# A hand-written order in place of a greedy scheduler for the attention and routing steps

## The chip, the core and the metric

The kernel runs on one core of one Trainium2 chip. The metric is the device time of one execution in microseconds, from the first to the last instruction and what lies around it. Three runs of the kernel before gave 416.49, 416.77 and 417.19 us.

## What is computed

Three layers follow one another. `A` is attention with a window of 64 keys over 2 batches, 8 heads, 576 positions and a head size of 64; its output is 1152 tokens of 512. `B` is a mixture of 8 experts: each token goes to the expert of its largest logit, in order of token up to 288 per expert, and its result is scaled by the softmax weight. `C` is a dense layer of 2048.

```python
scores = q @ k.T / 8; scores = where(0 <= i - j < 64, scores, -1e9)
x = softmax(scores) @ v                                # 1152 x 512
logits = x @ w_gate; e = argmax(logits); gate = softmax(logits)[e]
y = gate * (relu(x @ w1[e]) @ w2[e])                   # first 288 tokens of an expert
h = y @ w_in; out = (h * clip(h + 3, 0, 6) / 6) @ w_out
```

## The kernel before

**Stages.** Attention works on 9 blocks of 128 tokens (`j`), each in two halves of 64 queries (`g`, 18 of them). After five blocks an *early routing* picks one expert, the one most chosen so far, from the logits of the first 640 tokens, so that its weights are loaded and its tokens gathered while attention goes on. When all nine blocks are done the *late routing* places all tokens. Then TensorE works off the rest of the early expert's units, the teams of experts, and the dense layer. The order of everything from the early expert's remaining units on comes from a second planner in the same file with an estimate of its own; the change does not touch it.

**Steps of the first part.** Each is a node with a name, an engine or two it may run on, a cost, what it needs, a ring of buffers it takes from, and those that it frees:

- `lq`, `lk`, `lv` j: load 128 rows of q, k, v (256 KB each; block 4 crosses from one batch to the next, so its loads are two transfers). They are issued on SP's queue, one after the other, and so are `wg` (gate weights, two small transfers), `st` (store of a finished block) and `wl` u h (eight loads of 512 KB of the early expert's weights).
- `tq`, `tk`, `tv` j: TensorE turns the rows, four 128x128 products into one bank (L504). `eq`, `ek`, `ev`: ScalarE or VectorE copies the bank out (`copy`, L456 to L462).
- `s` j: 16 score products of 64x64 into two banks (L568). `m` g: VectorE adds the mask and takes the maximum, four instructions (L581). `e` g: four exponentials on ScalarE (L594). `pt` g: the turn of the result (L604); `ep` g: its copy.
- `cv0` to `cv2` j: GpSimd copies v into place (L486). `gw` j: the gate logits of v, four products (L534). `ew`, `tw`, `ex`: copied, turned (L548), copied beside v.
- `av` j: 16 products with the values (L622) into one pair of banks; `f` j: VectorE divides and sums up the logits (`finish`, L634 to L650).
- Early routing: `top` (`choose`, L130 to L138), `pp` (counts), `pl` (`early_expert`), `fl` (`early_flags`), `gE` (`early_gate`), `ix` and `ie` (index), `ga` (GpSimd gathers 128 rows), `sE`, `tE`, `xE` (scaled, turned, copied), `hotp`.
- The early expert: `e0`, `e1` u (two halves of the first product), `er` (relu), `et`, `eh` (turned, copied), `e2`, `e3` (second product).
- Late routing: `ch`, `cn`, `pL`, `rk`, `sa`, `px`, `sx`, `g0` (first gather), `gt`, `gc`, `hot`, `pg`, `sg`.

Rings matter where a step waits: `sp` (1) lets `s` j+1 begin only when both masks of block j are done; `p` (1) is the one bank of the `pt`; `x` (1) is one bank shared by `gw`, `tw`, `pp`, `ix`, `tE` and others; `t` (2) the two banks of the turns; `o` (1) the pair of banks of `av`.

**What sets the order.** `run_nodes` (L424) keeps a clock for each engine, looks at all nodes whose needs are met, and issues next the one with the smallest key: its start by the clock, a priority from the table `PRIO`, and its cost. Nodes with two engines get the one that comes out ahead. The engines then run their instructions in the order in which they were issued; each engine waits where an operand is not there.

Of the kernel before, what the change touches and what calls it, by code (L numbers as in the profile page):

```python
# [23 lines left out]
def tile_kernel(ctx, tc, q, k, v, w_gate, w1, w2, w_in, w_out, out, cap):  # L24
# [292 lines left out]
    GAP = -0.2  # L317
    EPS, CW, COLD, LAG = 0.015, 0.3, 6.0, 0.15
    PRIO = {'q': -30, 'k': -29, 'v': -27, 'tq': -7, 'eq': 8, 'tk': -10, 'ek': 3, 'cv': 1, 'tv': 1, 'ev': 2, 'gw': 1, 'ew': 1, 'tw': 1, 'ex': -4, 's': 2, 'm': 5, 'e': 2, 'pt': 2, 'ep': 9, 'av': 2, 'f': 8, 'st': 0, 'top': -5, 'tail': 2, 'ear': 78, 'hot': 60, 'gt': 25, 'fl': 13, 'ga': 58, 'xE': 5, 'turn': 20}
    CS = {'xE': 1.15, 'ep': 1.07, 'eq': 1.07, 'sE': 1.15, 'rk': 1.3, 'q': 1.15, 'v': 0.7}  # L320
    with ExitStack() as actx:
# [74 lines left out]
        nodes, done, emitted = {}, {}, []  # L396
# [3 lines left out]
        clock = dict.fromkeys(("PE", "A", "V", "P", "D"), 0.0)  # L400

        def node(name, prio, engs, fn, needs=(), take=None, free=(), lag=LAG):
            engs = {e: c * CS.get(name[0] if isinstance(name, tuple) else name, 1.0) for e, c in engs.items()}
            nodes[name] = (prio, engs, fn, needs, take, free, lag)

        def ready(name):
            _, _, _, needs, take, _, _ = nodes[name]
            r = 0.0
            for n in needs:
                if n not in done:  # L410
                    return None
                r = max(r, done[n])
            if take:
                order = taken[take]
                if len(order) >= rings[take]:
                    old = order[len(order) - rings[take]]
                    if freed.get((take, old), (0, 0.0))[0] < holders.get((take, old), 1):
                        return None
                    r = max(r, freed[take, old][1])
            return r  # L420

        holders, now = {}, [0.0]

        def run_nodes():  # L424
            while nodes:
                able = []
                for name, (prio, engs, *_) in nodes.items():
                    r = ready(name)
                    if r is None:
                        continue  # L430
                    for e, c in engs.items():
                        t = max(clock[e], r)
                        if e == "PE" and t < COLD:
                            c = 2 * c
                        key = (t + EPS * prio + (c if len(engs) > 1 else min(engs.values())) * CW, prio)
                        able.append((key, name, e, t, c))
                best = min(able)

                able = [a for a in able if a[3] + a[4] <= best[3] + GAP]
# [222 lines left out]
        node("wg", 6, {"D": 0.3}, lambda e: load_wg(), lag=2.0)  # L662
        node("rc", 30, {"P": 6.0}, lambda e: routing_constants())
        A_V = {"A": 0.5, "V": 0.6}
        for j in range(NJ):
# [20 lines left out]
            old = [("av", i) for i in (j - NV, j - NV + 1) if i >= 0]
            node(("ex", j), p + PRIO["ex"], {"A": 0.32, "V": 0.4}, x_out(j), [("tw", j)] + old, None, [("x", ("tw", j))])
            for g in (2 * j, 2 * j + 1):
                o = p + g % 2
# [184 lines left out]
        node("top", p, {"V": 0.8}, lambda e: choose(0, NE), [("f", j) for j in range(NE)] + ["rc"])  # L874
        node("pp", p, {"PE": 0.3}, early_counts, ["top"], "x")
        node("pl", p, {"V": 1.4}, early_expert, ["pp"], None, [("x", "pp")])
        node("fl", p + PRIO["fl"], {"V": 1.2}, early_flags, ["pl"])
        node("gE", p + PRIO["fl"], {"V": 1.35}, early_gate, ["fl"])
        node("ix", p + PRIO["fl"], {"PE": 0.2}, early_index, ["gE"], "x")
        node("ie", p + PRIO["fl"], {"V": 0.3}, early_index_out, ["ix"], None, [("x", "ix")])  # L880
        node("ga", p + PRIO["ga"], {"P": 1.04}, early_gather, ["ie"], lag=6.0)
        node("sE", p + PRIO["turn"], {"A": 0.48, "V": 0.4}, early_scale, ["ga"])
        node("tE", p + PRIO["turn"], {"PE": 0.44}, early_turn, ["sE"], "x")
# [1210 lines left out]
```

## Time and profile before

| | us |
|---|---|
| median of 3 runs (lowest, highest) | 416.77 (416.49, 417.19) |
| the profiled execution | 416.61 |
| its span, first to last instruction | 414.9 |
| PE busy | 400.3 (96% of the span) |
| DVE busy | 280.1 (68%) |
| ACT busy | 233.9 (56%) |
| POOL busy | 49.3 (12%) |

PE is TensorE, DVE VectorE, ACT ScalarE, POOL GpSimd, SP the engine that issues most transfers. The span is measured by the profiler inside one execution, so a change of the span by some us is one of the time. Matmuls are pipelined: the busy time of one is longer than the step from its start to the start of the next, and it is the steps that add up. The mean granted clock of TensorE over the span was 0.994 of full speed.

### The profile page before, as it was taken

What the parts mean: (1) busy time and instruction counts of PE and PEld (TensorE: products, weight loads), DVE (VectorE), ACT (ScalarE), POOL (GpSimd) and SP (SyncE); (2) the same over time, 40 slices, a digit from 0 to 9 for tenths busy, and PEclk for the clock granted to TensorE, in tenths of its full rate; (3) what the DMA queues carried; (4) which work ended last, traced back from release to release, by engine and by line L of the source; (5) the groups of instructions that cost most, each with busy time, mean ns of one, the idle gap of its engine ahead of it and who ended that gap; (6) DMA issues with size and microseconds to landing.
All of it is one profiled execution on the core that took longest, in us unless ns stands there. A gap on an engine that the chain in (4) does not pass through costs nothing.

```text
span 414.9 us, 8440 instructions
## 1 busy us (share of the span) xinstructions
PE 400.3 (96%) x3066; PEld 341.7 (82%) x3066; DVE 280.1 (68%) x781; ACT 233.9 (56%) x510; POOL 49.3 (12%) x109
## 2 busy tenths in 40 slices
PE   8999889999999999999999999999999999999992
PEld 5787666668999898898989999888888888999981
DVE  1988977599789789876789999358895222322430
ACT  3886863687586747666885566267573222322330
POOL 8733402030012000000000000000000000200111
PEclk9999999999999999999999999999999999999997
DMA  9999685987787999899700560033500000100101
GB/s 168 212 217 222 218 294 171 308 285 240 228 263 226 352 300 303 286 344 346 263 2 0 165 242 0 2 101 103 203 2 2 0 0 2 74 27 2 51 28 57
DMA packets 63842, 65.43 MB, mean 158 GB/s; under 512 B 30688, under 2 KB 47072, under 8 KB 63792
## 3 DMA queue, kind: packets, MB, share of 16 engines
q1 hardware_dynamic: 62224, 59.79, 46.4%
q0 software_dynamic: 1568, 5.01, 3.6%
q8 instruction: 26, 0.43, 0.4%
q14 instruction: 24, 0.20, 0.1%
HBM read 60.08 MB, written 4.72 MB: 156 GB/s over the span
## 4 chain that ended last, share of the span: by engine, by line
PE 90%; DVE 5%; ACT 2%; issue 1%; POOL 0%; POOLq 0%; ACTq 0%; DVEq 0%
PE banks L244 76%; PE banks L504 2%; PE banks L622 2%; PE banks L568 1%; PE banks L604 1%; DVE neg L581 1%; PE banks L1475 1%; PE banks L661 1%; PE banks L1500 1%; PE banks L534 1%; PE banks L1310 1%; ACT pe L594 1%; PE banks L1559 1%; PE banks L1408 0%; DVE xt L649 0%
## 5 line engine op out<-in xcount | busy, mean ns | idle before, releaser
L244 PE MATMUL banks<-x,wt 128*128 128x320 f32 (+3 forms) x432 | 79.8, 336 | 0.0
L244 PEld LDWEIGHTS banks<-x,wt 128*128 128x128 f32 x432 | 70.8, 188 | 7.1
L244 PE MATMUL banks<-wt,g 128*128 128x512 f32 x288 | 69.6, 390 | 0.0
L263 DVE TENSOR_TENSOR wt<-raw,wt 128x512 fp32r<-128x512 f32 x100 | 64.6, 685 | 4.9 <-ACT wt L258 4.6
L1621 DVE SCALAR_TENSOR_TENSOR gf<-r,banks 128x320 f32<-128x320 f32 (+3 forms) x48 | 26.6, 553 | 60.3 <-ACT r L1618 60.1
L1618 ACT ACTIVATE r<-banks,c_three 128x320 f32<-128x320 f32 (+3 forms) x48 | 27.9, 582 | 68.4 <-PE banks L244 68.2
L244 PEld LDWEIGHTS banks<-wt,g 128*128 128x128 f32 x288 | 53.7, 188 | 10.6
L258 ACT CAST wt<-raw 128x512 fp32r<-128x512 f32 x100 | 58.7, 628 | 4.5 <-PE banks L244 4.0
L244 PE MATMUL banks<-xT,wt 128*128 128x224 f32 (+2 forms) x288 | 38.2, 282 | 0.0
L244 PE MATMUL banks<-h,wt 128*128 128x224 f32 (+2 forms) x288 | 37.0, 279 | 0.0
L244 PEld LDWEIGHTS banks<-xT,wt 128*128 128x128 f32 x288 | 34.8, 191 | 1.6 <-issue 0.4
L244 PEld LDWEIGHTS banks<-h,wt 128*128 128x128 f32 x288 | 34.6, 192 | 0.8 <-issue 0.8
L1624 ACT CAST g<-gf 128x320 fp32r<-128x320 f32 (+2 forms) x40 | 21.3, 534 | 16.4 <-DVE gf L1621 16.4
L1627 DVE TENSOR_TENSOR g<-gf,g 128x320 fp32r<-128x320 f32 (+2 forms) x40 | 23.3, 584 | 10.1 <-ACT g L1624 9.4
L1664 POOL DMA_INDIRECT out_dram<-raw,cidx x4 | 3.9, 981 | 204.5 <-DVE raw L1658 196.9
L244 PE MATMUL banks<-x,wt_fixed 128*128 128x320 f32 (+3 forms) x144 | 26.8, 337 | 0.4 <-ACT x L1391 0.4
L244 PEld LDWEIGHTS banks<-x,wt_fixed 128*128 128x128 f32 x144 | 23.5, 188 | 3.0 <-ACT x L1391 0.7
L206 ACT ACTIVATE c<-raw 128x512 f32<-128x512 f32 x32 | 21.5, 673 | 6.2 <-DVE raw L229 4.7
L244 PE MATMUL banks<-wt_fixed,g 128*128 128x512 f32 x96 | 23.2, 390 | 0.0
L222 DVE SCALAR_TENSOR_TENSOR c<-raw,c 128x512 uint32<-128x512 uint32 x32 | 22.1, 690 | 0.8
L581 DVE CUSTOM_DVE_ANT_0 neg<-banks,tmask 128x128 f32<-128x128 f32 x72 | 16.2, 286 | 9.4 <-PE banks L568 9.4
L594 ACT ACTIVATE pe<-neg,nmx 128x128 f32<-128x128 f32 x72 | 22.3, 392 | 0.1
(310 smaller groups left out, 629.4 us busy)
## 6 DMA issues: line engine op xcount, KB each, us to landing
raw<-in_moe_w_dram SPq DMA_DIRECT2D x56, 512.0 KB, 5.9
raw<-in_moe_w_in_dram SPq DMA_DIRECT2D x16, 512.0 KB, 6.6
raw<-in_moe_w_out_dram SPq DMA_DIRECT2D x16, 512.0 KB, 6.1
early<-in_moe_w_dram SPq DMA_DIRECT2D x8, 512.0 KB, 6.6
x_dram<-xt SPq DMA_DIRECT2D x9, 256.0 KB, 2.8
q_sb<-in_q_dram SPq DMA_DIRECT2D x8, 256.0 KB, 3.9
k_sb<-in_k_dram SPq DMA_DIRECT2D x8, 256.0 KB, 4.8
v_sb<-in_v_dram SPq DMA_DIRECT2D x8, 256.0 KB, 4.5
```

The lines of the kernel that those rows point to most:

```text
L206: nc.scalar.activation(box["c"].bitcast(F32), box["hi"].bitcast(F32), AF.Abs)
L222: nc.vector.scalar_tensor_tensor(out=box["c"], in0=box["hi"], scalar=0xC0000000, in1=box["c"], op0=ALU.bitwise_and, op1=ALU.bitwise_or,)
L244: nc.tensor.matmul(out, l, r, start=(start and n == 0), stop=(stop and n == len(pairs) - 1))
L258: nc.scalar.copy(hi, r)
L263: V.tensor_tensor(out=lo, in0=r, in1=hi.bitcast(F32), op=ALU.subtract)
L504: nc.tensor.transpose(pt[:, hp, :], t[:, 2 * hp : 2 * hp + 2, :].rearrange("p h d -> p (h d)"), ident)
L581: V.tensor_tensor_reduce(out=neg[:, hp, :], in0=box["sp", g][:, hp, :], in1=tmask[:, first, :], scale=-1.0, scalar=3.0e38, op0=ALU.add, op ...
L594: nc.scalar.activation(pe[:, hp, :], neg[:, hp, :], AF.Exp, bias=nmx[:, hp : hp + 1], scale=-1.0)
L1618: nc.scalar.activation(r, ph, AF.Relu, bias=c_three)
L1621: V.scalar_tensor_tensor(out=gf, in0=r, scalar=6.0, in1=ph, op0=ALU.min, op1=ALU.mult)
L1624: nc.scalar.copy(hi, gf)
L1627: V.tensor_tensor(out=lo, in0=gf, in1=hi.bitcast(F32), op=ALU.subtract)
```

## The change

The greedy choice is gone. One string, `ATTENTION`, lists the 309 steps in the order in which they are issued, with `:a` or `:v` behind those that may run on ScalarE or VectorE. `run_nodes` goes through it word by word. Priorities, the tables `PRIO` and `CS`, the names `holders` and `GAP` and the counting of holders are gone; node costs are other numbers, and each engine's clock starts at another time. The steps themselves, their rings and their instructions are the same; 30 of the copies are on the other of their two engines.

```diff
-    GAP = -0.2
-    EPS, CW, COLD, LAG = 0.015, 0.3, 6.0, 0.15
-    PRIO = {'q': -30, 'k': -29, 'v': -27, 'tq': -7, ...
-    CS = {'xE': 1.15, 'ep': 1.07, 'eq': 1.07, 'sE': 1.15, 'rk': 1.3, 'q': 1.15, 'v': 0.7}
+    ATTENTION = """
+        lk.0 tk.0 ek.0:a lq.0 lv.0 cv2.0 lq.1 tq.0 lk.1 tv.0 eq.0:a s.0 m.0 m.1 lv.1 cv1.0 tq.1 ev.0:a eq.1:a wg
...
+        f.8 ch hotp.1 e0.1 e1.0 pL cn rk er.0:a e1.1 er.1:a hotp.3 et.0 et.1 st.6 eh.0:a e0.2 sa hot.6 e2.0 px hot.8
+        sx eh.1:v e3.0 e1.2 gt er.2:v e2.1 hot.5 hot.7 gc e3.1 g0 pg sg
+    """
...
-        clock = dict.fromkeys(("PE", "A", "V", "P", "D"), 0.0)
+        clock = {"PE": 5.0, "A": 1.3, "V": 1.2, "P": 7.1, "D": 2.9}
...
         def run_nodes():
-            while nodes:
-                able = []
-                for name, (prio, engs, *_) in nodes.items():
...
-                best = min([best] + able, key=lambda a: (a is best, a[0][1])) if able else best
-                _, name, e, t, c = best
-                _, _, fn, _, take, free, lag = nodes.pop(name)
+            name_of = {n if isinstance(n, str) else ".".join(map(str, n)): n for n in nodes}
+            for word in ATTENTION.split():
+                word, _, e = word.partition(":")
+                name = name_of.pop(word)
+                engs, fn, _, take, free, lag = nodes[name]
+                e = {"a": "A", "v": "V"}[e] if e else next(iter(engs))
+                t, c = max(clock[e], ready(name)), engs[e]
+                if e == "PE":
+                    if t < 7.1:
+                        c *= 1.95
...
                 if take:
                     taken[take].append(name)
                 now[0] = t
                 fn(e)
                 clock[e] = t + c
-                done[name] = t + c + lag
+                done[name] = t + c + (LAG[e] if lag is None else lag)
...
-            node(("s", j), o + PRIO["s"], {"PE": 0.93}, scores(j), needs, "sp", [("qd", ("eq", j))])
+            node(("s", j), {"PE": 0.9}, scores(j), needs, "sp", [("qd", ("eq", j))])
```

**VectorE, early routing.** The election of the early expert ends with `eI`; the rows of `neg` and `nmx` are a mask group (numbers tell the buffers apart). Before:

```order
L743 TENSOR_REDUCE e1_1_216<-e8_0_211 128x1
L744 TENSOR_SCALAR nsub_131<-subE_128 128x8
L745 CAST eI_222<-e1_1_216 128x1
L581 ISA neg_1001,nmx_1002<-banks_84,tmask_170 128x128
L581 ISA nmx_1002 128x1
```

Now:

```order
L744 TENSOR_REDUCE e1_1_216<-e8_0_211 128x1
L745 TENSOR_SCALAR nsub_131<-subE_128 128x8
L746 CAST eI_222<-e1_1_216 128x1
L756 TENSOR_TENSOR top_f_88<-oh_87,subE_128 128x40
L757 TENSOR_SCALAR capS_130<-subE_128 128x8
```

The flags follow the election at once; the mask groups that stood between `top`, `pl`, `fl` and `gE` stand ahead of `f.4` and `top`, except those of blocks 7 and 8, which stand behind `gE` as before.

**SP, the loads after the gate weights.** `wgb` is `wg`; a row with x2 and 64 partitions is a load of block 4 in two halves. Before:

```order
L359 DMA wgb_177<-in_moe_w_gate_dram 64x4x8 x2
L472 DMA q_sb_303<-in_q_dram 128x8x64
L472 DMA k_sb_327<-in_k_dram 128x8x64
L472 DMA v_sb_351<-in_v_dram 128x8x64
L472 DMA q_sb_378<-in_q_dram 128x8x64
L472 DMA k_sb_406<-in_k_dram 128x8x64
L472 DMA v_sb_441<-in_v_dram 128x8x64
```

Now:

```order
L373 DMA wgb_177<-in_moe_w_gate_dram 64x4x8 x2
L478 DMA k_sb_288<-in_k_dram 64x8x64 x2
L478 DMA k_sb_299<-in_k_dram 128x8x64
L478 DMA q_sb_337<-in_q_dram 128x8x64
L478 DMA q_sb_348<-in_q_dram 128x8x64
L478 DMA k_sb_365<-in_k_dram 128x8x64
L478 DMA v_sb_378<-in_v_dram 128x8x64
```

The loads k.4, k.2, q.2, q.3, k.3, v.2 stand where q.2, k.2, v.2, q.3, k.3, v.3 stood; v.3, q.4 and k.7 follow. Behind them SP has `lv.4 lk.5 lq.5 lv.5 lq.6 lk.8 st.0 lk.6 lq.7 st.1 st.2 lv.6 lv.7 lq.8 st.4 lv.8 st.3`, then seven of the weight loads `wl`, `st.5`, and the eighth.

**ScalarE, the end of attention.** `pe` are the exponentials of a half block, `pT` and `vT` copies of turned banks, `vx` and `vy` the copies `ex`, `c64` the scaling `sE` of the gathered rows. Before, the last instructions of attention:

```order
L460 COPY pT_1145<-banks_84 128x512
L460 COPY vT_1154<-banks_84 128x512
L594 ACTIVATE pe_1190<-neg_1173,nmx_1174 128x128 x4
L460 COPY vx2_187<-banks_84 128x8x8
L460 COPY vy2_190<-banks_84 64x8x8
L594 ACTIVATE pe_1218<-neg_1182,nmx_1183 128x128 x4
L460 COPY pT_1252<-banks_84 128x512
L594 ACTIVATE pe_1276<-neg_1246,nmx_1247 128x128 x4
L594 ACTIVATE pe_1285<-neg_1254,nmx_1255 128x128 x4
L462 ACTIVATE c64_1188<-c64_1188,sgE_133 128x512
L460 COPY pT_1310<-banks_84 128x512
```

Now:

```order
L466 COPY vT_1141<-banks_84 128x512
L600 ACTIVATE pe_1188<-neg_1083,nmx_1084 128x128 x4
L600 ACTIVATE pe_1193<-neg_1143,nmx_1144 128x128 x4
L466 COPY pT_1226<-banks_84 128x512
L600 ACTIVATE pe_1236<-neg_1181,nmx_1182 128x128 x4
L466 COPY pT_1241<-banks_84 128x512
L466 COPY vx1_186<-banks_84 128x8x8
L466 COPY vy1_189<-banks_84 64x8x8
L466 COPY vy2_190<-banks_84 64x8x8
L600 ACTIVATE pe_1260<-neg_1200,nmx_1201 128x128 x4
L468 ACTIVATE c64_1179<-c64_1179,sgE_133 128x512
L466 COPY pT_1305<-banks_84 128x512
```

Between the exponentials of the last four half blocks stand two copies `pT` (ep.14, ep.15) and the three of ex.7, where one `pT` and the two of ex.8 stood; the scaling `c64` is still ahead of the last `pT`.

## Rows read from the trace of the kernel before

**Rows 1.** The page's chain of work that ended last: shares by engine.

```profile
PE 90%; DVE 5%; ACT 2%; issue 1%; POOL 0%; POOLq 0%; ACTq 0%; DVEq 0%
```

**Rows 2.** Busy time by stretch (length; then busy of each engine, clock, DMA share, GB/s).

```profile
7.90:36.93 29.03, 28.56 (x483) 23.16 (x484) 23.85 (x128) 22.27 (x65) 15.11 (x45) 1.00 0.97 210
36.93:61.14 24.21, 20.90 (x362) 16.10 (x361) 20.99 (x140) 18.61 (x54) 6.67 (x12) 1.00 0.83 264
61.14:72.86 11.72, 10.82 (x77) 7.57 (x74) 8.27 (x45) 3.55 (x14) 3.33 (x5) 1.00 0.49 154
72.86:414.90 342.04, 333.70 (x2129) 291.39 (x2127) 226.59 (x467) 186.89 (x374) 17.71 (x17) 0.99 0.43 146
```

**Rows 3.** The chain in order of time, one block of attention (start, us, what).

```profile
20.45 1.18 PE banks L622 x32
...
22.22 0.87 PE banks L504 x8
23.09 1.03 PE banks L568 x32
...
24.71 0.35 PE banks L534 x8
25.07 0.59 PE banks L504 x4
25.66 0.16 PE banks L548
```

**Rows 4.** VectorE's timeline from the end of av.4 to the masks of block 7.

```profile
36.93 0.17 DVE L634 TENSOR_SCALAR rd<-banks 128x8 f32<-128x8 f32 x1 [0.68 <-PE banks L622]
...
38.40 0.20 DVE L130 TENSOR_REDUCE top_m<-logits 128x5 f32<-128x40 f32 x1
...
39.61 0.28 DVE L581 CUSTOM_DVE_ANT_0 neg<-banks,tmask 128x128 f32<-128x128 f32 x1
...
41.30 0.15 DVE L733 SCALAR_TENSOR_TENSOR e<-banks,c_desc 128x8 f32<-128x8 f32 x1
...
42.54 0.28 DVE L581 CUSTOM_DVE_ANT_0 neg<-banks,tmask 128x128 f32<-128x128 f32 x1
...
43.38 0.20 DVE L755 TENSOR_TENSOR top_f<-oh,subE 128x40 f32<-128x40 bf16 x1
...
45.11 0.28 DVE L581 CUSTOM_DVE_ANT_0 neg<-banks,tmask 128x128 f32<-128x128 f32 x1
...
45.95 0.19 DVE L770 TENSOR_REDUCE et<-ex 128x5 f32<-128x40 f32 x1
...
47.88 0.21 DVE L456 COPY vx<-banks 128x64 f32<-128x64 f32 x1
...
50.78 0.28 DVE L581 CUSTOM_DVE_ANT_0 neg<-banks,tmask 128x128 f32<-128x128 f32 x1
```

**Rows 5.** DMA issues around 6.3, 11.55, 12.94 and 51.2 us (last: us to landing).

```profile
wgb<-in_moe_w_gate_dram SPq DMA_DIRECT2D x1, 8.0 KB, 4.0
...
k_sb<-in_k_dram SPq DMA_DIRECT2D x1, 256.0 KB, 5.9
...
v_sb<-in_v_dram SPq DMA_DIRECT2D x1, 256.0 KB, 5.6
...
c<-x_dram,eI POOLq DMA_INDIRECT x1, 7.1
```

**Rows 6.** SP's timeline: the issues of the eleventh and twelfth load.

```profile
11.55 1.11 SPq L472 DMA_DIRECT2D k_sb<-in_k_dram  x1
12.94 0.87 SPq L472 DMA_DIRECT2D v_sb<-in_v_dram  x1
```

**Rows 7.** ScalarE's timeline from 45.48: exponentials of two half blocks, two copies.

```profile
45.48 2.45 ACT L594 ACTIVATE pe<-neg,nmx 128x128 f32<-128x128 f32 x8
47.83 0.56 ACT L460 COPY kT<-banks 128x512 f32<-128x512 f32 x1
48.30 0.59 ACT L462 ACTIVATE qd<-banks 128x512 f32<-128x512 f32 x1
```

More of the change, by code (lines that the diff above doesn't have):

```diff
@@ L392, in rows @@
                 o += n
-        nodes, done, emitted = {}, {}, []
+        nodes, done = {}, {}
         rings = {'q': 3, 'k': 4, 'v': 3, 'qd': NQD, 't': 2, 's': 2, 'sp': 1, 'p': 1, 'o': 1, 'x': 1, 'neg': 4, 'pe': 3, 'pT': 4, 'vT': 3, 'vw': 4, 'xt': 4}
@@ L399, in tile_kernel, with node @@
         freed = {}
-        clock = dict.fromkeys(("PE", "A", "V", "P", "D"), 0.0)
-        def node(name, prio, engs, fn, needs=(), take=None, free=(), lag=LAG):
-            engs = {e: c * CS.get(name[0] if isinstance(name, tuple) else name, 1.0) for e, c in engs.items()}
-            nodes[name] = (prio, engs, fn, needs, take, free, lag)
+        clock = {"PE": 5.0, "A": 1.3, "V": 1.2, "P": 7.1, "D": 2.9}
+        def node(name, engs, fn, needs=(), take=None, free=(), lag=None):
+            nodes[name] = (engs, fn, needs, take, free, lag)
         def ready(name):
-            _, _, _, needs, take, _, _ = nodes[name]
+            _, _, needs, take, _, _ = nodes[name]
             r = 0.0
             for n in needs:
-                if n not in done:
-                    return None
                 r = max(r, done[n])
@@ L415, in ready @@
                 if len(order) >= rings[take]:
[L416 to L419, printed above, removed]
-            return r
-        holders, now = {}, [0.0]
+                    r = max(r, freed[take, order[len(order) - rings[take]]])
+            return r
+        now, form = [0.0], [128]
+        FORMS = {"gw": 32, "s": 64, "av": 73}
+        LAG = {"PE": 0.2, "V": 0.14, "A": 0.15, "P": 0.1, "D": 1.5}
         def run_nodes():
-            while nodes:
-                able = []
-                for name, (prio, engs, *_) in nodes.items():
[L428 to L439, printed above, removed]
-                best = min([best] + able, key=lambda a: (a is best, a[0][1])) if able else best
-                _, name, e, t, c = best
-                _, _, fn, _, take, free, lag = nodes.pop(name)
+            name_of = {n if isinstance(n, str) else ".".join(map(str, n)): n for n in nodes}
[8 more added lines that the diff above has]
+                        c *= 1.95
+                    f = FORMS.get(word.split(".")[0], 128)
+                    if f != form[0]:
+                        form[0] = f
+                        c += 0.094
                 if take:
@@ L447, in run_nodes @@
                 clock[e] = t + c
-                done[name] = t + c + lag
+                done[name] = t + c + (LAG[e] if lag is None else lag)
                 for ring, owner in free:
-                    n, was = freed.get((ring, owner), (0, 0.0))
-                    freed[ring, owner] = n + 1, max(was, t + c + 0.1)
+                    freed[ring, owner] = max(freed.get((ring, owner), 0.0), t + c + 0.15)
+            assert not name_of, name_of
         def copy(e, out, in_, scale=None):
@@ L686, in tile_kernel @@
+            node(("gw", j), {"PE": 0.18}, v_gate(j), [("ev", j), "wg"], "x", [("vT", ("ev", j))])
+            node(("ew", j), {"A": 0.17, "V": 0.2}, w_out_(j), [("gw", j)], "vw", [("x", ("gw", j))])
+            node(("tw", j), {"PE": 0.11}, w_turn(j), [("ew", j)], "x", [("vw", ("ew", j))])
             old = [("av", i) for i in (j - NV, j - NV + 1) if i >= 0]
-            node(("ex", j), p + PRIO["ex"], {"A": 0.32, "V": 0.4}, x_out(j), [("tw", j)] + old, None, [("x", ("tw", j))])
+            node(("ex", j), {"A": 0.16 * parts, "V": 0.2 * parts}, x_out(j), [("tw", j)] + old, None, [("x", ("tw", j))])
@@ L702, in tile_kernel @@
                 needs += [("ex", j - 1), ("cv2", j - 1)]
-            node(("av", j), p + PRIO["av"], {"PE": 1.15}, values(j), needs, "o", free)
+            node(("av", j), {"PE": 1.1}, values(j), needs, "o", free)
             if j + 1 < NJ:
-                node(("f", j), p + PRIO["f"], {"V": 1.3}, lambda e, j=j: finish(j), [("av", j)], "xt", [("o", ("av", j))])
-                node(("st", j), p + PRIO["st"], {"D": 0.62}, lambda e, j=j: store_x(j), [("f", j)], None, [("xt", ("f", j))])
-            else:
-                node(("f", j), p + PRIO["f"], {"V": 0.85}, lambda e, j=j: finish(j), [("av", j)])
-        p = 10 * NE + PRIO["top"]
+                node(("f", j), {"V": 1.35}, lambda e, j=j: finish(j), [("av", j)], "xt", [("o", ("av", j))])
+                node(("st", j), {"D": 0.75}, lambda e, j=j: store_x(j), [("f", j)], None, [("xt", ("f", j))])
+            else:
+                node(("f", j), {"V": 1.0}, lambda e, j=j: finish(j), [("av", j)])
         A1E = ac.tile([128, NE, 128], F16, name="A1E")
@@ L872, in early_out @@
             copy(e, t, box["aE"])
[L874 to L883, printed above, removed]
+        node("top", {"V": 1.2}, lambda e: choose(0, NE), [("f", j) for j in range(NE)] + ["rc"])
+        node("pp", {"PE": 0.3}, early_counts, ["top"], "x")
+        node("pl", {"V": 1.25}, early_expert, ["pp"], None, [("x", "pp")])
+        node("fl", {"V": 1.75}, early_flags, ["pl"])
+        node("gE", {"V": 1.9}, early_gate, ["fl"])
+        node("ix", {"PE": 0.2}, early_index, ["gE"], "x")
+        node("ie", {"V": 0.3}, early_index_out, ["ix"], None, [("x", "ix")])
+        node("ga", {"P": 0.4}, early_gather, ["ie"], lag=6.0)
+        node("sE", {"A": 0.61, "V": 0.5}, early_scale, ["ga"])
+        node("tE", {"PE": 0.44}, early_turn, ["sE"], "x")
         node(
-            "xE", p + PRIO["xE"], {"A": 0.48, "V": 0.6}, lambda e: copy(e, xTE, box["tE"]), ["tE"], None,
+            "xE", {"A": 0.5, "V": 0.6}, lambda e: copy(e, xTE, box["tE"]), ["tE"], None,
             [("x", "tE")],
```

98 lines of the change are left out of this document (50 added, 48 removed).

## The prediction

> **What bounds the kernel now.** I read the chain of waits first, to see which engine the end hangs on: TensorE has 90% of it [rows 1]. Then the busy time in five stretches, cut where the chain changes hands [rows 2]. The reader should compare PE busy with the length of each stretch. From 72.86 us on TensorE is busy 333.70 of 342.04, and most of the rest is the last store. Between 7.90 and 36.93 it idles 29.03 − 28.56 = 0.47 us, between 36.93 and 61.14 it idles 3.31, between 61.14 and 72.86 it idles 0.90. The change reaches only what lies before 72.86: the instructions behind it stand as they stood. So the gain can come from two places: the 4.68 us of idling, and the returns of TensorE from another array shape, which [rows 3] price. Four 128x128 turns take 0.44 (the row of x8 is 0.87), but 0.59 when they follow the values, scores or gate products. That is 0.15 for each return.
>
> Third I read the timeline of VectorE from 36.93 [rows 4], because there DVE rows stand in the chain. The reader should see the early routing cut in slices: `top` at 38.40, two mask groups, `pl` at 41.30, a mask group, `fl` at 43.38, a mask group, `gE` at 45.95, and the next masks (m.14) only at 50.78. In these 12.38 us VectorE is the bound; TensorE, ScalarE and the loads wait for it.
>
> Below, a name such as m.14 is a step of the list: m masks of a half block, e exponentials, pt and ep turn and copy of them, s scores, av values, f finish, tq/tk/tv turns, ew/ex copies of the gate part.
>
> **The change, part by part.**
>
> *Durations, clocks, the removed priorities.* Nothing. With order and engine both written, no duration decides where an instruction stands.
>
> *Up to `top`.* Now 36.93 is where av.4 ends, and `top` starts at 38.40 [rows 4]. In the list av.4 has two more scores in front of it (s.5, s.6: 2 × 1.03), one single turn less (0.16) and three returns less (11 in place of 14, because s.3 gw.2 av.1, gw.3 av.2, gw.4 av.3 and s.6 gw.5 av.4 now stand side by side): 2.06 − 0.16 − 0.45 = +1.45 us, so 38.4 minus the idling of before that may vanish, about 37.9. Next the waits that the list makes. The gate weights are issued with the same place in the queue and land at 6.3 + 4.0 [rows 5]; gw.0 now stands right behind two turns and can begin at 10.05, so it waits 0.3 to 0.5. The loads k.4 (in two halves) and then k.2, q.2, q.3, k.3, v.2, v.3 follow the first six. The eleventh and twelfth load land at 11.55 + 5.9 = 17.45 and 12.94 + 5.6 = 18.54 [rows 5, 6], 1.09 apart; the 210 GB/s of [rows 2] make 262 kB in 1.25. I take 1.18, between them. Counted back, q.2 lands at 15.0 and q.3 at 16.2, and TensorE reaches them 0.3 us earlier each. Counted on, the eighteenth, q.5, lands at 25.6, where TensorE stands at 25.2: 0.4. With 0.3 behind the VectorE copy ew.0 I have 1.7 us of waits and av.4 ending at 39.6. VectorE has m.12 and m.13 in front of f.4, which end at 39.8; f.4 takes 1.47 (36.93 to 38.40), so `top` starts at 41.3, **+2.9 us**. Bounds: no wait at all gives 37.9 + 1.47 = 39.4, twice the waits 43. All later loads have slack: v.6 waits in SP's queue for the store behind f.2 (about 32.3), lands near 37 and is turned at 39.6; v.8 waits for the store behind f.4, lands near 45.5 and is turned at 49.5.
>
> *From `top` to m.14.* The four mask groups have gone in front of f.4, and the slices stand together. `top` 1.21 (38.40 to 39.61), ep.10 0.6 (no row of it here; ScalarE's copy of a tile of that size lasts 0.56 to 0.59 [rows 7]), 0.3 of waiting for the counts, `pl` 1.24, `fl` 1.73, `gE` 1.93 [rows 4]: 7.0 us in place of 12.38. Then m.14 starts at 48.3 instead of 50.78, **−5.4**. Cover: s.7 must be done by then. TensorE has 6.5 us of work from av.4 to s.7 by the prices of [rows 3], and waits about 1.1 us, because tw.6 and av.5 stand behind the bank that `pl` frees; s.7 ends at 47.2, a microsecond early.
>
> *From m.14 to the end of av.8.* Before, 50.78 to 61.14 = 10.36. What is late next is ScalarE. It has ep.12, ev.8, e.14, e.15, ep.14, e.16, ep.15, ex.7, e.17, sE, ep.17 in this order. A copy of a bank moves it on by 0.47 (47.83 to 48.30), two groups of exponentials by 2.35 (45.48 to 47.83) [rows 7]: 5 × 0.47 + 4 × 1.18 + about 1.15 for ex.7 and sE (0.59 is the longest copy of [rows 7]) = 8.2. ep.12 cannot start before TensorE has done pt.13, gw.7, tq.8 and pt.12 behind s.7, about 1.2 after m.14 starts. Behind ep.17 come its remaining length, a hop and av.8 (1.18): 1.4. About 0.9 is spent waiting, ev.8 for its turn and sE for the gathered rows. Sum 11.7, **+1.3**: bound from below by 10.8 (no wait), above by the gather (rivals). av.8 ends at 60.0 where it was 61.14.
>
> *The tail.* The same instructions follow in another order: e0.0 e0.1 e1.0 cover the last routing step, where two halves did. TensorE idled 0.90 of 11.72 [rows 2]. Bounds 0 and 0.90; ScalarE still scales the last tile ahead of er.0, so I keep half: **−0.45**. GpSimd's gathers and SP's raw loads hang on the slot index in this tail and come about as much earlier. They have over 15 us until TensorE has worked off the early expert's own units.
>
> Sum: +2.9 − 5.4 + 1.3 − 0.45 = −1.6 us against the profiled execution's 416.61: 415.0. That execution lies 0.16 below the median of 416.77, so I say **415.2**.
>
> **A rule on the gather.** In the kernel before, the gather of the early rows was issued at 51.2, with six weight loads in front of it, and took 7.1 to land [rows 5]. In the list seven weight loads (issued 45.5 to 49.5, as `pl` ends at 44.5) stand right in front of it, at 50.3. If it took the same 7.1, it lands at 57.4, just when sE wants it; this is what I assume. At the 264 GB/s of [rows 2] the seven loads need 14 us from 45.5 on; if the gather comes with the last of them, it lands at 59.5, and the sum gives 417.3.
> The Trainium skill, "DMA: Bandwidth & Descriptors", on queue arbitration, says that each DMA engine round-robins between its queues a packet at a time. By that rule the rows, which are on a queue of their own, need not wait for the loads: the time stays 415.2, and rival 2 loses its chance; whether 7.1 us with six loads in front was such sharing, no row here shows.
>
> **Rivals.**
> *1. The waits for loads don't come* (chance 0.25). The pace is 1.09, and TensorE reaches av.4 at its work bound: `top` at 39.4, 1.9 us earlier: 413.3. For it: between 7.90 and 36.93 all idling of TensorE is 0.47 us, so the loads kept up. Against: the new order loads k.4 and k.7 before they are due.
> *2. The gather is late* (0.12). sE stands in front of ep.17 on ScalarE, ep.17 in front of av.8 on TensorE. Landing at 59.5 in place of 57.4 costs 2.1: 417.3, no difference. For it: the seven loads; against: the 7.1 of before, under a like load.
> *3. Nothing comes through* (0.09). The front is shorter, but the weight loads of the next stage, which hang on the slot index, keep their time, and TensorE waits for them: 416.8. Against: the slack of over 15 us named above.
> *4. Slower: the loads fall behind* (0.14). The place is tq.5: all of TensorE's work stands behind the eighteenth load, and tk.6 behind the twenty-third transfer. At a pace of p the eighteenth comes 6 × (p − 1.18) later, the twenty-third 11 × (p − 1.18) less 1.5 of slack. The forecast of −1.6 turns into +0.83 from p = 1.54 on. At 1.6 the loss is 3.1: 418.3. For it: k.4 comes in halves of 64 partitions, among the loads that are late anyway, and stores share the queue. Against: 1.54 us would be 170 GB/s, and the stretch as a whole had 210.
>
> **How the numbers follow.** A measurement of this kernel can tell about 0.2% from no change, 0.83 us. The forecast has 0.40, with 414.2 to 415.9 as its own range. Faster: forecast and rival 1, 0.65. Same: rivals 2 and 3, 0.21. Slower: rival 4, 0.14. The range goes from 412.6 (rival 1, with the waits for the counts and of the tail gone too) to 417.5 (rival 2 with its price rounded up), and leaves out rival 4 and a little below.
>
> **What would show it.** Right: VectorE's L130 rows begin near 41.3, `top` to the first masks behind `gE` takes some 7 us without a mask group between, TensorE's last values end near 60.0 and the first turn of the tail's end (72.86 before) stands near 71.2. TensorE's waits before 40 us name DMA, gate weights among them. ScalarE is without long gaps from 50 to 59. Wrong: `top` before 40 (rival 1); a wait of ScalarE for the gathered tile (rival 2); 71.2 met but the total unchanged (rival 3); `top` after 44 with loads as releaser (rival 4).

## The result and the profile after

The changed kernel is slower: 420.80 us (419.99 to 421.77, 4 runs) against 416.79 for the kernel before, measured beside it. The ratio is 1.0096, 95% interval 1.0073 to 1.0120, so 4.0 us were lost where 1.6 were forecast to be gained.

| profiled execution | before | after |
|---|---|---|
| its own time, us | 416.61 | 420.68 |
| span, us | 414.9 | 419.0 |
| PE busy | 400.3 (96%) | 400.0 (95%) |
| mean granted clock of TensorE | 0.994 | 0.986 |

First the busy time in stretches, cut at the marks that answer to those of before [rows 2]: the end of av.4, the end of av.8, and the first turn of the planner behind (L1982 in this kernel; the lines of the attention part stand 6 lower in the file than before, L622 is now L628). Columns: length, then busy time of PE, PEld, DVE, ACT, POOL, TensorE's granted clock, DMA share, GB/s.

```profile
7.90:40.50 32.60, 29.50 (x541) 24.14 (x532) 24.57 (x146) 26.65 (x80) 14.09 (x45) 1.00 0.94 196
40.50:65.92 25.42, 20.43 (x303) 16.85 (x299) 17.81 (x111) 16.85 (x51) 8.02 (x14) 0.87 0.69 229
65.92:76.75 10.83, 10.57 (x75) 7.41 (x74) 8.18 (x44) 2.89 (x12) 2.63 (x4) 1.00 0.53 172
76.75:419.00 342.25, 333.80 (x2135) 291.51 (x2130) 227.38 (x470) 186.99 (x374) 18.68 (x18) 0.99 0.44 146
```

The last stretch is what it was, 342.25 against 342.04. Nearly all of the loss lies ahead of 76.75, where 72.86 stood: +3.89. The second stretch is the odd one: TensorE is idle for 5 us of it, and its mean clock is 0.87.

VectorE's timeline gives the marks between (start, length, what):

```profile
40.79 0.16 DVE L640 TENSOR_SCALAR rd<-banks 128x8 f32<-128x8 f32 x1
42.25 0.20 DVE L130 TENSOR_REDUCE top_m<-logits 128x5 f32<-128x40 f32 x1
44.37 0.17 DVE L734 SCALAR_TENSOR_TENSOR e<-banks,c_desc 128x8 f32<-128x8 f32 x1
45.62 0.19 DVE L756 TENSOR_TENSOR top_f<-oh,subE 128x40 f32<-128x40 bf16 x1
47.34 0.19 DVE L771 TENSOR_REDUCE et<-ex 128x5 f32<-128x40 f32 x1
49.00 0.28 DVE L587 CUSTOM_DVE_ANT_0 neg<-banks,tmask 128x128 f32<-128x128 f32 x1
```

Against [rows 4]: `top` at 42.25 for 38.40, from `top` to the mask m.14 6.75 us for 12.38, so m.14 is 1.78 earlier than before. Up to here the change wins. What it loses behind, the waits of TensorE name (total, how often, longest):

```profile
PE banks L628 <- POOL vy L492: 3.2, 1, 3.2
PE banks L510 <- DMA q_sb<-in_q_dram: 2.2, 3, 1.2
...
PE banks L540 <- DMA wgb<-in_moe_w_gate_dram: 0.8, 1, 0.8
```

The values product (L628) waits 3.2 us for `vy`, a copy on GpSimd (L492, a `cv` step). GpSimd's timeline shows why:

```profile
48.53 0.95 POOL L892 TENSOR_TENSOR A1t<-A,c_tok 128x128 f16<-128x128 f16 x2 [5.25 <-DVE rhsE L779]
50.65 1.19 POOL L800 DMA_INDIRECT c<-x_dram,eI  x1 [1.16 <-DVE sgE L795]
51.88 0.41 POOL L892 TENSOR_TENSOR A1t<-A,c_tok 128x128 f16<-128x128 f16 x1
58.38 1.30 POOL L492 TENSOR_SCALAR vy<-v_sb 64x512 f32<-64x512 f32 x2 [6.09 <-DMA c<-x_dram,eI]
59.76 0.62 POOL L492 TENSOR_SCALAR vx<-v_sb 128x512 f32<-128x512 f32 x1
```

The two copies at 58.38 are cv2.7 and cv2.6. They stand behind the gather `ga`, and GpSimd is idle for 6.09 us until the gathered tile `c` has landed. The copies use nothing of that tile, but the wait is in the program. Here are GpSimd's instructions with what each waits for (`c64` is the gathered tile, DMASW the gather's own signal). The wait is listed for cv2.7 (`vy2`); cv2.6 (`vy1`) has none of its own and is held because it stands behind it:

```
L800 DMA c64_1179<-x_dram_80,eI_222 128x512 [waits DMAHW5_49,DMAHW4_49,DMAHW6_49,DMAHW2_49,DVE_49]
L892 TENSOR_TENSOR A1t_94<-A1_93,c_tok_73 128x128
L492 TENSOR_SCALAR vy2_190<-v_sb_835 64x8x64 [waits DMASW0_49,PE_49,Pool_49]
L492 TENSOR_SCALAR vy1_189<-v_sb_817 64x8x64
```

In the kernel before, all copies stood ahead of `ga`. Now TensorE (start, length, what, idle time before) and its clock in steps of 2 us:

```profile
56.24 0.28 PE L554 MATMUL banks<-ident,vw 128*128 128x128 f32 x1
59.73 0.38 PE L628 MATMUL banks<-vy,pT 128*64 128x73 f32 x1 [3.22 <-POOL vy L492]
...
61.88 1.12 PE L610 MATMUL banks<-ident,pe 128*128 128x128 f32 x4
62.79 1.06 PE L815 MATMUL banks<-ident,c 128*128 128x128 f32 x4
...
65.92 2.86 PE L244 MATMUL banks<-early 128*128 128x256 f32 x12
```

```profile
56.00:58.00 2.00, 0.52 (x5) 0.30 (x3) 1.02 (x4) 1.41 (x5) 0.00 (x0) 1.00 1.02 371
58.00:60.00 2.00, 0.27 (x4) 0.27 (x6) 0.00 (x0) 0.72 (x1) 1.48 (x3) 0.77 1.04 387
60.00:62.00 2.00, 2.00 (x33) 1.85 (x32) 0.00 (x1) 0.00 (x0) 1.68 (x4) 0.50 0.73 258
62.00:64.00 2.00, 2.00 (x12) 1.67 (x14) 1.47 (x6) 0.59 (x1) 0.00 (x0) 0.50 0.03 9
64.00:66.00 2.00, 2.00 (x33) 1.85 (x31) 0.58 (x1) 0.00 (x0) 0.00 (x0) 0.52 0.38 139
66.00:68.00 2.00, 2.00 (x10) 1.77 (x11) 1.68 (x9) 1.21 (x7) 0.00 (x0) 1.00 0.00 0
```

In the pause the granted clock falls to 0.50, the level of 1.2 GHz, and comes back only at 66. av.7 goes from 59.73 to 61.88, 2.15 us where one took 1.18 [rows 3]; av.8 is as slow. So one wait is paid twice.

### The profile page after: what moved, and what is told of

It is laid out like the page before. It is cut to its first block, busy times and chain, and to the rows that moved or that the text cites. A ratio compares the mean times of both kernels' runs of the same rounds, so it can differ in the third digit from the quotient of the medians.

```text
span 419.0 us, 8433 instructions
## 1 busy us (share of the span) xinstructions
PE 400.0 (95%) x3066; PEld 342.8 (82%) x3066; DVE 278.4 (66%) x772; ACT 236.2 (56%) x519; POOL 49.9 (12%) x109
## 3 DMA queue, kind: packets, MB, share of 16 engines
q0 software_dynamic: 1568, 5.01, 3.6%
## 4 chain that ended last, share of the span: by engine, by line
PE 88%; DMA 5%; SPq 2%; DVE 1%; ACT 1%; issue 1%; POOL 0%; POOLq 0%; ACTq 0%; DVEq 0%
PE banks L244 76%; DMA q_sb<-in_q_dram 3%; PE banks L628 2%; DMA c<-x_dram,eI 2%; PE banks L510 1%; PE banks L610 1%; SPq L478 1%; PE banks L574 1%; PE banks L1473 1%; PE banks L1498 1%; DMA wgb<-in_moe_w_gate_dram 1%; PE banks L1308 1%; PE banks L1557 1%; PE banks L1406 0%; PE banks L1435 0%
```

## The experiments

Theory 1: the loss is the place of the copies behind the gather, by the wait of av.7 and by the clock. Theory 2, the rival: it is the new order of the loads, for which TensorE waits 2.8 us ahead of 40 us (0.8 for the gate weights, 0.8 and 1.2 for q.3 and q.5). All ratios are to the kernel before, run on the same chip.

| kernel | us | ratio, 95% interval |
|---|---|---|
| changed kernel | 420.80 | 1.0096 (1.0073 to 1.0120) |
| e1 copies first | 415.40 | 0.9965 (0.9951 to 0.9979) |
| e2 pause filled | 418.51 | 1.0042 (1.0027 to 1.0057) |
| e3 loads | 420.03 | 1.0072 (1.0056 to 1.0089) |
| e4 copies and loads | 414.93 | 0.9956 (0.9939 to 0.9973) |
| e5 masks between | 417.80 | 1.0016 (1.0006 to 1.0025) |
| e6 weight loads behind | 414.09 | 0.9930 (0.9913 to 0.9946) |
| e7 scaling last | 415.94 | 0.9970 (0.9957 to 0.9982) |
| e8 one copy | 416.92 | 1.0006 (0.9986 to 1.0027) |
| e9 gates later | 414.13 | 0.9944 (0.9927 to 0.9961) |
| e10 tail back | 416.41 | 0.9983 (0.9974 to 0.9992) |
| e11 weight loads alone | 415.20 | 0.9960 (0.9948 to 0.9972) |

**e1, the copies first.**

```diff
-        eq.8:a wl.3.0 wl.1.0 ix ie tv.8 ep.12:a wl.3.1 cv1.6 hotp.2 ev.8:a m.15 gw.8 hotp.4 s.8 f.5 wl.0.0 ga m.16
-        hotp.0 e.14 e.15 cv2.7 cv2.6 m.17 pt.14 av.6 ep.14:a wl.0.1 pt.15 ew.8:v cv0.8 e.16 ep.15:a tw.7 ex.7:a f.6
+        eq.8:a wl.3.0 wl.1.0 ix ie tv.8 ep.12:a wl.3.1 cv1.6 cv2.6 cv2.7 hotp.2 ev.8:a m.15 gw.8 hotp.4 s.8 f.5 wl.0.0 ga m.16
+        hotp.0 e.14 e.15 m.17 pt.14 av.6 ep.14:a wl.0.1 pt.15 ew.8:v cv0.8 e.16 ep.15:a tw.7 ex.7:a f.6
```

> The two value copies cv2.6 and cv2.7 go ahead of hotp.2 on GpSimd, so ahead of the gather; nothing else moves. Theory 1 (the copies wait for the gather's landing; av.7 waits 3.2 us for them, and the pause drops TensorE's clock): no wait of L628 for vy, granted clock 1.00 from 56 to 66 us, av.7 from about 56.5, av.8 ends near 60.8 in place of 66.0, so 5.2 us less than the changed kernel's 420.8: 415.6. Theory 2 (the loss comes from the loads that TensorE waits for before 40 us): the order behind stays as late, 420 or above.

Measured 415.40. GpSimd's and TensorE's timelines of e1:

```profile
47.12 0.69 POOL L492 TENSOR_SCALAR vy<-v_sb 64x512 f32<-64x512 f32 x1 [3.31 <-PE banks L628]
...
50.71 1.19 POOL L800 DMA_INDIRECT c<-x_dram,eI  x1 [0.80 <-DVE sgE L795]
51.94 0.41 POOL L892 TENSOR_TENSOR A1t<-A,c_tok 128x128 f16<-128x128 f16 x1
52.31 0.63 POOL L492 TENSOR_SCALAR vx<-v_sb 128x512 f32<-128x512 f32 x1
```

```profile
56.51 0.28 PE L628 MATMUL banks<-vy,pT 128*64 128x73 f32 x1
...
60.56 2.86 PE L244 MATMUL banks<-early 128*128 128x256 f32 x12
```

The gather is issued at the same time, av.7 starts at 56.51 without a wait, and the early expert's first product, which stands right behind av.8, starts at 60.56 in place of 65.92: 5.36 us, the whole gain. A copy of block 8 still stands behind the gather here and runs at 52.31 without waiting for it. So it is not every copy that is given the wait: in the changed kernel it is cv2.7, and why the program has it there is not settled.

The edit has a price of its own. VectorE in e1 and, second fence, in the changed kernel, at the same place and at m.14:

```profile
47.08 0.79 DVE L750 TENSOR_SCALAR A1E<-c_i128h,et 128x128 f16<-128x128 f16 x2
49.43 0.28 DVE L587 CUSTOM_DVE_ANT_0 neg<-banks,tmask 128x128 f32<-128x128 f32 x1
```

```profile
47.02 0.41 DVE L750 TENSOR_SCALAR A1E<-c_i128h,et 128x128 f16<-128x128 f16 x2
49.00 0.28 DVE L587 CUSTOM_DVE_ANT_0 neg<-banks,tmask 128x128 f32<-128x128 f32 x1
```

The two L750 (steps of the early routing) take 0.79 us beside the GpSimd copy of 47.12 and 0.41 without it (0.41 also in e8, where that copy is not there). L137, part of `top`, takes 0.44 for 0.20 beside the other copy that was moved. From `top` (42.06) to m.14 e1 takes 7.37 us for 6.75, so its gather is issued no earlier though `top` came 0.19 earlier.

**e2, the pause filled.**

```diff
                 box["pr", j] = pr
+                if j == 7:
+                    for _ in range(14):
+                        nc.tensor.matmul(pw, warm[:, 0:128], warm, start=True, stop=True)
                 for h in range(H):
```

> 14 bf16 products of 128x512 on TensorE, with no use, stand right ahead of av.7 and fill the pause; everything waits as before. Theory 1: av.7 still starts near 59.7, behind the gather, but at a granted clock of 1.00; av.7, the turns and av.8 then take 3.5 instead of 6.2 us: 2.7 less than 420.8, so 418.1. If the pause alone is the loss and the clock costs nothing, 420.8.

Measured 418.51. The same steps of 2 us, in e2:

```profile
58.00:60.00 2.00, 1.83 (x23) 0.92 (x22) 0.00 (x0) 0.68 (x1) 1.74 (x3) 1.00 1.05 394
60.00:62.00 2.00, 1.74 (x32) 1.42 (x26) 1.17 (x5) 0.58 (x1) 1.41 (x4) 1.00 0.47 164
62.00:64.00 2.00, 1.83 (x35) 1.73 (x36) 1.27 (x6) 0.00 (x0) 0.00 (x0) 1.00 0.35 131
```

The clock stays at 1.00. av.7 starts at 59.47, as late as before the edit, and the early expert's product at 63.34: 3.87 us where it took 6.19. This is 2.3 us, and the times differ by 420.80 − 418.51 = 2.3 as well. The rest to e1, 418.51 − 415.40 = 3.1, is the wait itself. The loss is split: 3.1 by the wait, 2.3 by the clock.

The Trainium skill, "TensorE: Matmul & The Clock Gate", Part 1, says that a gate lets through only part of TensorE's clock pulses, by how busy the engine has been. These two runs agree: same instructions at 0.50 behind a pause, at 1.00 where useless products fill it.

**e3 and e4, the loads,** without and with e1's edit.

```diff
-        lk.4 tk.1 gw.0 lk.2 tv.1 ek.1:a cv0.0 ev.1:v e.0 s.1 ew.0:v e.1 lq.2 tw.0 pt.0 tk.4 lq.3 m.3 ex.0:v tk.2
-        ep.0:a lk.3 pt.1 cv1.1 m.2 lv.2 ep.1:v ek.4:a ek.2:a cv2.1 cv0.1 tq.2 gw.1 eq.2:a tq.3 s.2 e.2 eq.3:v m.4
-        lv.3 e.3 lq.4 tk.3 pt.2 cv1.2 ep.2:a e.4 av.0 pt.3 lk.7 ep.3:a ew.1:v ek.3:v tw.1 tv.3 m.5 ev.3:a tq.4 pt.4
+        tk.1 gw.0 lk.2 tv.1 ek.1:a cv0.0 ev.1:v e.0 s.1 ew.0:v e.1 lq.2 tw.0 pt.0 lq.3 m.3 ex.0:v tk.2
+        ep.0:a lk.3 pt.1 cv1.1 m.2 lv.2 ep.1:v ek.2:a cv2.1 cv0.1 tq.2 gw.1 eq.2:a tq.3 s.2 e.2 eq.3:v m.4
+        lv.3 e.3 lq.4 lk.4 tk.3 pt.2 cv1.2 ep.2:a e.4 av.0 pt.3 ep.3:a ew.1:v ek.3:v tw.1 tv.3 m.5 ev.3:a tq.4 pt.4
...
```

Behind it `tk.4` follows `ep.4`, `ek.4` follows `s.3`, and `lk.7` follows `lq.6`.

> Loads k.4 and k.7 go back behind q.4 and q.6 (the turn and copy of k.4 with them); GpSimd's order stays. Theory 1: the waits for q.3 and q.5 (2.0 us) vanish, top starts near 40.2 instead of 42.25, the gather and all behind it come as much earlier, but the copies still stand behind the gather: 418.8, slower than before. Theory 2: 416.5 or below.

> Both edits, of e1 and e3. Theory 1: 5.2 and 2.0 add up, 413.6, below both kernels. Theory 2: as e3, 416.5 or below with e1's edit worth nothing.

Measured 420.03 and 414.93: theory 2 falls, for the loads alone give 0.8, and 0.5 beside e1 (in both cases the intervals overlap). But both were sized wrong by theory 1, which had 2.0. In both `top` comes at 40.71, 1.5 earlier than in the changed kernel, where 40.2 was expected. The gather's landing does not follow. ScalarE's scaling of the gathered rows (`sE`) in e3 and, second fence, in e4:

```profile
57.98 0.72 ACT L468 ACTIVATE c<-c,sgE 128x512 f32<-128x512 f32 x1 [2.07 <-DMA c<-x_dram,eI]
```

```profile
57.06 0.72 ACT L468 ACTIVATE c<-c,sgE 128x512 f32<-128x512 f32 x1 [0.92 <-DMA c<-x_dram,eI]
```

e3 issues the gather 1.5 us earlier than the changed kernel (49.12 for 50.65) and scales at 57.98 for 58.23: the rows were on their way for 8.9 us there, by the scaling that waits for them. The waiting copies come with it, and TensorE's wait for `vy` grows to 4.5. So the next bound was the gather's landing, which e6 tries.

**e5, two mask groups back.** From e1, `m.12` goes behind `top` and `m.13` behind `pl`.

```diff
-        ex.4:a s.6 gw.5 f.3 ep.9:a m.12 m.13 av.4 tv.6 e.10 ew.5:a tw.5 ev.6:a pt.10 ex.5:a f.4 lq.8 tq.7
-        cv0.6 eq.7:a gw.6 tk.7 ew.6:a top tv.7 ek.7:a pp e.12 ep.10:v tk.8 pt.11 cv0.7 cv1.7 pl tw.6 fl st.4 ep.11:a
+        ex.4:a s.6 gw.5 f.3 ep.9:a av.4 tv.6 e.10 ew.5:a tw.5 ev.6:a pt.10 ex.5:a f.4 lq.8 tq.7
+        cv0.6 eq.7:a gw.6 tk.7 ew.6:a top m.12 tv.7 ek.7:a pp e.12 ep.10:v tk.8 pt.11 cv0.7 cv1.7 pl m.13 tw.6 fl st.4 ep.11:a
```

> From e1 (copies first, 415.4), the mask group m.12 goes back behind top and m.13 behind pl. In e1 VectorE has no gap from 38.9 (m.12) to 56; av.4 ends near 40.3 there. If it is the order of VectorE that carried the gain (it fills its wait for av.4 with masks), it now idles about 1.4 us ahead of f.4 and everything behind m.14 is that much later: 416.9, the time of the kernel before. If only the gather or ScalarE bounds the stretch behind, 415.4.

Measured 417.80, 2.4 above e1 where 1.5 was expected. VectorE in e5, at f.4 and at m.14:

```profile
40.41 0.17 DVE L640 TENSOR_SCALAR rd<-banks 128x8 f32<-128x8 f32 x1 [1.81 <-PE banks L628]
41.88 0.20 DVE L130 TENSOR_REDUCE top_m<-logits 128x5 f32<-128x40 f32 x1
...
51.07 0.28 DVE L587 CUSTOM_DVE_ANT_0 neg<-banks,tmask 128x128 f32<-128x128 f32 x1
```

It now idles 1.81 us ahead of f.4 (1.4 was expected), `top` starts only 0.2 earlier than in e1, and m.14 starts at 51.07, 1.64 later. The gather, issued at 52.36 for 50.71, also took 8.2 in place of 7.3. So the gain from VectorE's new order is real: two mask groups cost 1.8 us between the slices (9.19 from `top` to m.14 for 7.37) and nothing ahead of f.4, where VectorE waits for av.4 anyway.

**e6, e9 and e11, the weight loads around the gather.** e6 starts from e4, e9 from e6, e11 from e1. In e6 and e11, where the `wl` words also leave all their other places:

```diff
-        av.5 ev.7:a s.7 e.13 ex.6:a gE cv2.5 lv.8 m.14 ek.8:a pt.13 st.3 gw.7 wl.2.1 ep.13:a ew.7:a tq.8 pt.12
+        av.5 ev.7:a s.7 e.13 ex.6:a gE cv2.5 lv.8 m.14 ek.8:a pt.13 st.3 gw.7 wl.0.0 wl.1.0 wl.0.1 ep.13:a ew.7:a tq.8 pt.12
...
+        pt.16 tw.8 e.17 sE:a av.7 ep.16:v cv1.8 ex.8:v pt.17 f.7 tE st.5 wl.1.1 wl.2.0 wl.3.0 wl.2.1 wl.3.1 ep.17:a xE:v av.8 e0.0 st.7
```

In e9 besides:

```diff
-        tk.1 gw.0 lk.2 tv.1 ek.1:a
+        tk.1 lk.2 tv.1 gw.0 ek.1:a
```

> From e4 (414.9), three weight loads (the two first halves and one second half that are used first) stay ahead of the gather, the other five go behind the store of block 5. Theory A (the gather shares its way with the seven loads in front): it takes much less than the 7.7 us of e4 and lands before 55, so the scaling no longer waits 0.9 and av.8 ends 0.9 earlier: 414.0. Theory B (7 us are the gather's own): it still takes 7 to 8 us and the time stays at 414.9.

> From e6 (414.1), the gate product gw.0 goes behind the turn tv.1, so that the 0.8 us wait for the gate weights is half covered. If the front end binds through VectorE (top follows av.4), top comes 0.4 earlier and the time is 413.7; if the stretch from 50 us on binds, 414.1.

> From e1 (415.4), only the weight loads move as in e6 (three ahead of the gather, five behind the store of block 5); the other loads stay as the change has them. If the gather's landing binds the end of attention, it takes 6.3 us in place of 7.1 and the scaling's wait of 0.5 goes: 414.9. If e6's gain came from the loads at the front, 415.4.

Measured 414.09, 414.13 and 415.20. The gather, issue to landing, in e6, e9 and e11, and behind them in e4 with seven loads in front:

```profile
c<-x_dram,eI POOLq DMA_INDIRECT x1, 6.3
```

```profile
c<-x_dram,eI POOLq DMA_INDIRECT x1, 4.7
```

```profile
c<-x_dram,eI POOLq DMA_INDIRECT x1, 5.0
```

```profile
c<-x_dram,eI POOLq DMA_INDIRECT x1, 7.7
```

With three loads in front it takes 4.7 to 6.3 us, with seven 7.3 to 8.9 (8.9 in e3; 7.3 to 8.2 in e1, e2, e4, e5, e7, e8, e10 and the changed kernel; in e2, e3 and e8 read from the scaling that waits for it). So the gather is theory A's, though in e6 it lands at 56.0 and not before 55, and the scaling no longer waits in any of the three. What it is worth is small: 0.8 from e4 to e6, 0.2 from e1 to e11, and in both cases the intervals overlap. e9's median is e6's, so its edit shows no gain, though `top` came at 40.55 for 41.05. Seven of the versions have an interval below the kernel before (e1, e4, e6, e7, e9, e10, e11); e6 is lowest, 0.7% below (0.5 to 0.9), the changed kernel 1.0% above it.

Small differences between single profiles are not the edits'. Kernels with the same order up to `top` differ there by 0.7 us (e3, e4, e6, e7: 40.71 to 41.43) and by 0.9 (the changed kernel, e1, e2, e8, e10, e11: 41.85 to 42.72).

**e7, the scaling last.**

```diff
-        pt.16 tw.8 e.17 sE:a av.7 ep.16:v cv1.8 ex.8:v pt.17 f.7 wl.1.1 tE st.5 ep.17:a xE:v av.8 e0.0 wl.2.0 st.7
+        pt.16 tw.8 e.17 av.7 ep.16:v cv1.8 ex.8:v pt.17 f.7 wl.1.1 st.5 ep.17:a sE:a av.8 tE xE:v e0.0 wl.2.0 st.7
```

> From e4 (414.9), the scaling of the gathered rows goes behind the last copy ep.17 on ScalarE, their turn and copy behind av.8. av.8 no longer hangs on the gather and ends near 58.8 in place of 59.6, but the early expert's first product starts near 60.0 in place of 59.6. If what follows av.8 (choose, ranks, slots) binds the tail: 414.2. If TensorE's work binds it: 415.3.

Measured 415.94, worse than either: the early expert's product starts at 61.18 for 59.60, because TensorE waits for the copy of the gathered rows (0.78) once nothing covers it. From there to L1982 it takes 10.83 us, as in the changed kernel. So TensorE's work binds the tail, not the routing behind av.8. Not all of the 1.0 is the edit's: `top` came 0.7 later in this run than in e4 (41.43), and the gather took 8.0.

**e8, one copy alone.** Of e1's edit only `cv2.6` goes ahead of `hotp.2`.

> The changed kernel with cv2.6 alone ahead of hotp.2; cv2.7 and the copies of block 8 stay behind the gather. Theory 1: av.7 hangs on cv2.6 and not on cv2.7, so the wait of 3.2 us and the drop of the clock go as in e1; av.8 hangs on the three copies behind the gather, which end near 60.3 where av.8 could start near 59.6: 416.1. If any copy behind the gather costs the same, 420.8.

Measured 416.92. TensorE's waits in e8:

```profile
PE banks L815 <- ACT c L468: 0.8, 1, 0.8
PE banks L628 <- POOL vy L492: 0.7, 1, 0.7
```

av.7 no longer waits; av.8 waits 0.7 for the copies that stay behind the gather, as expected, and the clock stays at 1.00. cv2.7 starts at 59.12 here, 0.15 behind the scaling that waits for the gathered rows, as in the changed kernel (58.38 and 58.23). Theory 1 had 416.1; `top` came at 42.72 in this run for 42.06 in e1, about the rest.

**e10, the tail.**

```diff
-        f.8 ch hotp.1 e0.1 e1.0 pL cn rk er.0:a e1.1 er.1:a hotp.3 et.0 et.1 st.6 eh.0:a e0.2 sa hot.6 e2.0 px hot.8
+        f.8 ch hotp.1 e0.1 pL cn e1.0 rk er.0:a e1.1 er.1:a hotp.3 et.0 et.1 st.6 eh.0:a e0.2 sa hot.6 e2.0 px hot.8
```

> From e1 (415.4), the half product e1.0 goes back behind the late counts, so two halves and not three stand between av.8 and the late places. If the tail's gain of 0.9 us comes from there, TensorE again waits 0.7 us for the relu copy in place of 0.3 and the time is 415.9 to 416.3; if not, 415.4.

Measured 416.41, but for another reason. The tail of e10, from av.8 to L1982:

```profile
61.18:72.27 11.09, 10.72 (x76) 7.48 (x74) 8.19 (x44) 2.89 (x12) 2.63 (x4) 1.00 0.59 195
```

It is 11.09 us long, 0.26 above e1's 10.83. The wait for the relu copy is not where the 0.26 are: it is 0.26 in both. In e10 it is the count products that wait for VectorE (L926 starts 0.39 behind the row of L924, in e1 0.12). The other 0.6 lies ahead of the tail: the gather took 7.8 us in place of 7.3, which the edit does not touch. So three halves ahead of the late counts are worth about 0.3 of the 0.9. Most of the rest is the wait for the relu copy, 0.75 in the kernel before, which e10 leaves at 0.26; which word of the list shortened it was not tried.

## Why the prediction was wrong

The sum was built of four terms, and the marks allow each to be checked (profiled executions; e1 in the last column shows the marks without the one fault).

| term | forecast | after | e1 |
|---|---|---|---|
| up to `top` | +2.9 | 42.25 − 38.40 = +3.85 | +3.66 |
| `top` to m.14 | −5.4 | 6.75 − 12.38 = −5.63 | 7.37 − 12.38 = −5.01 |
| m.14 to the end of av.8 | +1.3 | 16.92 − 10.36 = +6.56 | 11.13 − 10.36 = +0.77 |
| tail | −0.45 | 10.83 − 11.72 = −0.89 | −0.89 |
| sum | −1.65 | +3.89 | −1.47 |

**The step that failed** is "From m.14 to the end of av.8", +1.3. There the prediction said "What is late next is ScalarE" and counted ScalarE's eleven steps. GpSimd's queue was not gone through, though the list shows `ga` in front of `cv2.7 cv2.6`, a place no copy had before. The term came out at +6.56. The 5.26 between are the wait of av.7, 3.2, and the clock behind it, 2.3, as e1 and e2 show (5.5 together; without them, in e1, the term is 0.5 below the forecast).

**The sign would have been right.** With the two copies ahead of the gather, and nothing else changed, the time is 415.40, where 415.2 was predicted. That it comes so near is luck in part: in e1 the four terms miss by +0.8, +0.4, −0.5 and −0.4 us, which nearly cancel. One by one:

- *Up to `top`*, +2.9: mis-sized by 1 us. 1.7 us of waits were counted; TensorE waits 0.76 for the gate weights, 0.81 for q.3 and 1.23 for q.5, 2.8 in all. The load of k.7 ahead of q.5 is one of the costs that e3 takes away (`top` at 40.71).
- *`top` to m.14*, −5.4: right, 6.75 us for 7.0. e5 confirms the cause, with an addition: VectorE is busy for 6.54 of the 6.75 us, so what counts is that masks fill the wait ahead of f.4.
- *The gather*: it took 7.6 us for the assumed 7.1 [rows 5], and made ScalarE wait 0.79 us.
- *Tail*, −0.45: it was −0.89. TensorE's idle time went from 0.90 to 10.83 − 10.57 = 0.26, and e10 gives about 0.3 of the gain to the third half product, the step named.

**The rivals.** Rival 4, the loads, was the slower one, and it did not happen: its sign was `top` after 44. The one that did happen was not among them: that a transfer on GpSimd's queue holds up the copies behind it. Rival 2 had the gather late for ScalarE; its mechanism was there (e6, e9 and e11 shorten the gather by taking loads away), but small.

**The rule on the gather.** By the Trainium skill, "DMA: Bandwidth & Descriptors", on queue arbitration, the gather's rows take turns with the loads and need not wait until these are through. The runs are in line with sharing: fewer loads in front make it faster, 4.7 to 6.3 us for 7.3 to 8.9. And in the changed kernel the gather, issued at 50.65, landed at 58.25, ahead of two loads that were issued before it (at 49.02 and 49.63, 9.6 and 10.3 us to landing, so 58.6 and 59.9). But "the time stays 415.2" does not follow from it, since sharing has a price of its own, some 2 us here between three loads and seven.

## What to carry to other kernels

When steps are put into a written list, go through every engine's queue, not only the busy ones: an engine that is busy 12% of the span decided this result. For each transfer that an engine issues, ask what stands behind it on that engine, read the waits that the program lists for those instructions, and put what others need soon ahead of it. A pause of TensorE can be paid a second time in clock, here 3.1 us for the wait and 2.3 for the clock behind it; where a pause can't be removed, useless products in it can be worth their place (2.3 of 420.8 us here).

## What the runs showed of the hardware

- TensorE's granted clock fell from 1.00 to 0.50 (2.4 to 1.2 GHz) in a pause of 3.2 us (busy 0.52 and 0.27 of two stretches of 2 us) and was back at 1.00 from 66 us on; the engine had been busy all the time from 59.73. The longest pause of e5, 1.5 us, left it at 1.00.
- A gather on GpSimd's queue that takes 1.2 us to issue can hold that engine for 6.1 us more, if an instruction behind it has its landing among its waits; instructions without it ran on at once (52.31 in e1).
- The same gather, of 128 rows, took 4.7 to 8.9 us, by the number of weight loads around it and with a scatter between kernels that have the same loads in front of it: 7.3 and 7.8 in e1 and e10, 6.3 and 4.7 in e6 and e9.
- VectorE's f16 TENSOR_SCALAR pair of 128x128 took 0.79 us while a GpSimd copy of 64x512 ran (e1) and 0.41 without one (the changed kernel, e8).
